# Windowed attention with a gated convolution layer on one core: 256-byte query and key runs, a block turn with unbroken writes, bias and row minimum in one operation, and a new order of the period

## The chip, the cores and the metric

The kernel runs on one core of a Trainium2 chip. The core has TensorE (PE, with its weight loads listed as PEld), VectorE (DVE), ScalarE (ACT), GpSimd (POOL), and SyncE (SP), which here only issues transfers. The metric is the device time of one execution in microseconds (us). The kernel before takes 621.04 us, the median of 3 runs (620.53 to 621.98).

## The reference, cut to what matters

Eight batches of 576 tokens, 8 heads of 64. Attention looks back at most 127 tokens and has a slope per head. A layer with a 3-tap convolution as its gate follows.

```python
scores = scale * np.matmul(q, k.transpose(0, 1, 3, 2))          # scale = 1/8
mask = (rel >= 0) & (rel < window)                              # window = 128
scores = np.where(mask, scores + bias[None], -1000000000.0)     # bias = -slope * distance
scores = scores - np.max(scores, axis=-1, keepdims=True)
attn = np.exp(scores)
attn = attn / (np.sum(attn, axis=-1, keepdims=True) + 1e-09)
x = np.matmul(attn, v)                                          # heads side by side: 512 wide
h = np.maximum(x @ w_in, 0.0)                                   # 512 -> 1024
conv_out = conv_w[0] * h[t-1] + conv_w[1] * h[t] + conv_w[2] * h[t+1]
out = h * (1 / (1 + np.exp(-conv_out))) @ w_out                 # 1024 -> 512
```

## The kernel before, in words

The 4608 tokens are cut into 36 tiles of 128. A tile's 8 heads are two halves of 4 (`u` is 0 or 1). The layer behind the attention works on chunks of 256 tokens, four steps per chunk, each step on 256 of the 1024 inner features. Every product with full precision is three passes of TensorE over a high and a low part of the numbers.

A whole program is an opening (tiles 0 to 7, weights, the first ten steps), fourteen periods of two tiles and four steps, and a tail. The order within these is written out by hand as strings of short codes, which `emit` plays off with a tile number t (even, 8 to 34) and a step number. Each engine keeps that order, and waits stand only where data or a buffer need them. So an instruction that waits holds up all that is behind it on its engine. The codes that the text speaks of, with the lines of the kernel before:

- LD: query and key loads (line 281, issued by SP). TQ: the 32x32 block turn on DVE (line 349). HQ, LQ: high part on ACT (line 362) and low part on POOL (line 369) of the turned tile.
- S: scores of a tile on PE (line 388), into four PSUM banks. MP: the previous tile's scores put in where the window needs them (DVE, line 461). MB: scale and bias added (line 487, DVE). RM: the row minimum of four heads (line 491, DVE). From tile 8 on, MB works on two heads at a time and RM on four. For tiles 0 to 7 one fused operation per head (line 480) does bias and minimum together.
- X: exponential with row sum (ACT, line 496). N: sum plus a constant, reciprocal and multiply (DVE, lines 507, 508, 514). T: transpose on PE (line 527). RL: its copy out of PSUM (ACT, line 535). SEL: the two window halves (POOL, lines 541 and 544). AV: product with the values (PE, line 560). XH, XL, XF: high and low part of the result (ACT line 576, DVE line 582), and one column copied round the ring for tiles divisible by 4 (DVE, line 587).
- UH: first product of a step (PE, line 619). HH: relu (ACT, line 631). Z: middle tap (ACT, line 637). CA, CB: the two side taps (DVE, line 652). TH: tanh (ACT, line 659). GT: gate (DVE, line 667). GH, GL: high and low part of the gated value (ACT line 679, POOL line 687). D: second product (PE, line 721). OB: the output copied out of PSUM and stored (ACT line 737, SP line 738).

PSUM holds five banks for scores, first products, transposes and AV results together, one for the convolution, two for the output. Where a tile or chunk straddles two batches, MP has a second operation and CA, CB are cut in two pieces.

In a load before, partition c of a block holds the four tokens 4c to 4c+3, which are 1024 unbroken bytes in memory. The turn must then write token 4c+m to column 4c+m, so that its writes step by four words:

```python
out=blks[tt][:, i].rearrange("p i g b (c m) -> p (i g) m b c", m=NB),
in_=raws[tt][:, i].rearrange("p i g (m b r) -> p (i g) m b r", m=NB, r=BK),
```

Of the kernel before, what the change touches and what calls it, by code (L numbers as in the profile page):

```python
# [8 lines left out]
F32 = mybir.dt.float32  # L9
# [13 lines left out]
def tile_alibi_window_attention_conv_glu(  # L23
# [10 lines left out]
    nc = tc.nc  # L34
    B, H, S, D = q.shape
# [3 lines left out]
    HU = 4  # L39
# [9 lines left out]
    cpool = ctx.enter_context(tc.tile_pool(name="cpool", bufs=1))  # L49
# [25 lines left out]
    spin(7, ones)  # L75
    neg = cpool.tile([P, 1], F32, name="neg")
    nc.vector.memset(neg, NEG)
    pos = cpool.tile([P, 1], F32, name="pos")
    nc.vector.memset(pos, -0.125 * NEG)

    def mask_from(name, conds):
        m = apool.tile([P, P], F32, name=name + "_f", tag="e", bufs=4)
# [194 lines left out]
    def load_blocks(t, dst, src):  # L277
        for r, b, s, n in segments(t):
            for j in range(NB):
                u, a = divmod(j, 2)  # L280
                nc.sync.dma_start(
                    out=dst[j * BK + r // NB : j * BK + (r + n) // NB],
                    in_=src[b, u * HU + a : (u + 1) * HU : 2, s : s + n, :].rearrange("g (c m) d -> c g (m d)", m=NB),
                )

    def load(t):
        if t >= TURN:
            raws[t] = apool.tile([P, 2, NG, NB * D], F32, name=f"rqk{t}", tag="rqk", bufs=3)
            if t == TURN:
                raws[t - 1, "k"] = apool.tile([P, 2, NG, NB * D], F32, name=f"rk{t - 1}", tag="rqk", bufs=3)  # L290
# [35 lines left out]
    def qkT_out(t, u):  # L326
        to = qkT_of(t)[:, t % SLOTS, u]
        ps = pts.pop((t, u)) if t < SPLIT else pts[t, u]
        if t < FIRST:
            nc.scalar.activation(out=to[:, 0], in_=ps[:, 0], func=AF.Copy, scale=-0.125)  # L330
            nc.scalar.copy(out=to[:, 1], in_=ps[:, 1])
        else:
            nc.scalar.copy(out=to, in_=ps)

    def qkT_rest(t, u):
        ps, hi = pts.pop((t, u)), as32(qkT_of(t)[:, t % SLOTS, u])
        low = qkT_low[:, t % SLOTS, u]
# [178 lines left out]

    def normal_act(t, u):
# [230 lines left out]
    def qk_rest(t):  # L748
# [61 lines left out]
    D-2 Z0.0 Z0.1 RM0.0 X0.0.0 X0.0.1 UH1.1 UH1.0 MB0.1.1 CA0.0 LQ1 RM0.1 CA0.1 X0.1.0 N0.0 X0.1.1 HH1 D-1 CB0.0 T0.0  # L810
    RL0.0 N0.1 T0.1 S1.0 CB0.1 RL0.1 TH0 TQ2 GT0 MP1.0.0 MB1.0.0 MP1.1.0 SEL0.0 AV-1 MP1.1.1 MB1.1.1 SEL0.1 AV0 GH0
    GL0 D0 XH-1 OB-2 XL-1 Z1.1 Z1.0 XH0 HQ2 LQ2 CA1.0 MB1.1.0 CA1.1 XL0 XF0 RM1.1 X1.1.0 CB1.0 MP1.0.1 CB1.1 X1.1.1
    TH1 LD5 MB1.0.1 UH2.1 UH2.0 HH2 Z2.0 Z2.1 GT1 OB0 GH1 N1.1 RM1.0 X1.0.0 X1.0.1 CA2.0 CA2.1 CB2.0 CB2.1 UH3.1
    UH3.0 T1.1 N1.0 GL1 TH2 GT2 RL1.1 LV3 SEL1.1 D1 HH3 Z3.1 Z3.0 TQ3 GH2 GL2 T1.0 RL1.0 SEL1.0 CA3.0 CA3.1 XF-1
    CB3.0 CB3.1 OB1 TH3 GT3
# [44 lines left out]
```

## Time and profile before

| what | value |
|---|---|
| median of 3 runs | 621.04 us |
| the profiled execution | 620.64 us |
| its span, first to last instruction | 618.9 us |
| PE / DVE / ACT / POOL busy | 97% / 86% / 71% / 47% |
| granted TensorE clock | full in all slices |
| chain that ended last | PE 59%, DVE 27%, ACT 5%, issue 5% |
| transfers | 47.39 MB, mean 77 GB/s |

The span is 1.7 us shorter than the execution. Busy shares are means over the whole span. A PE that counts as busy is not always at its peak rate, since the ends of its pipelined matmuls are modelled. So the chain and single stretches have to be read beside it.

### The profile page before, as it was taken

Reading aid. Unit: us, or ns where it says so; the run is one execution under the profiler, and the core shown is the slowest. Engines: PE = TensorE matmul, PEld = TensorE weight load, DVE = VectorE, ACT = ScalarE, POOL = GpSimd, SP = SyncE. Lnnn points to the kernel's source line nnn. Section 1 sums busy time; section 2 is a strip of 40 time slices with the busy share of each in tenths; the row PEclk is TensorE's granted clock in tenths of the full one; section 3 lists DMA queues with packets and bytes.
Section 4 is the critical chain, followed back from the end, with each engine's and each line's share of the span. In section 5 each row is a group of like instructions: output and inputs, shape, how many; then the busy total and the mean of one; then the engine's idle time right before and its main releaser. Section 6 shows DMA issues by size and latency. Waiting matters only on the chain.

```text
span 618.9 us, 14937 instructions
## 1 busy us (share of the span) xinstructions
PE 598.1 (97%) x5497; PEld 521.0 (84%) x5497; DVE 533.0 (86%) x1268; ACT 436.8 (71%) x1214; POOL 291.5 (47%) x362
## 2 busy tenths in 40 slices
PE   8999999999999999989999999999999999999997
PEld 7678877888897789879888888898989788989996
DVE  7999998899989998999898898889898999888553
ACT  6999977567776666758685768667777676676653
POOL 2679347553445354445354544434444535352411
PEclk9999999999999999999999999999999999999999
DMA  8997332312311222222322222221321120100001
GB/s 208 245 252 191 96 86 70 103 33 76 83 33 54 69 70 69 69 69 64 76 69 69 70 53 77 58 73 46 85 78 38 52 68 35 37 35 1 35 1 68
DMA packets 82012, 47.39 MB, mean 77 GB/s; under 512 B 61052, under 2 KB 75412, under 8 KB 81940
## 3 DMA queue, kind: packets, MB, share of 16 engines
q1 hardware_dynamic: 81940, 46.45, 27.7%
q8 instruction: 43, 0.70, 0.5%
q14 instruction: 29, 0.24, 0.1%
HBM read 36.99 MB, written 9.44 MB: 75 GB/s over the span
## 4 chain that ended last, share of the span: by engine, by line
PE 59%; DVE 27%; ACT 5%; issue 5%; POOL 1%; DMA 1%; SPq 0%; DVEq 0%; ACTq 0%
PE p L619 21%; PE o L721 20%; DVE zp L652 10%; PE av L560 7%; PE sc L388 5%; DVE sc L461 4%; PE pa L527 3%; DVE e L514 2%; DVE z L667 2%; DVE e L487 2%; ACT zp L637 2%; PE p L614 1%; DVE blk L349 1%; DMA rqk<-in_k_dram 1%; DVE st L491 1%
## 5 line engine op out<-in xcount | busy, mean ns | idle before, releaser
L619 PE MATMUL p<-ring,wi 128*128 128x256 f32 x1088 | 198.5, 284 | 3.7 <-DVE ring L587 3.7
L652 DVE SCALAR_TENSOR_TENSOR zp<-hh,cw,zp 128x256 f32<-128x256 f32 (+7 forms) x384 | 161.2, 420 | 28.8 <-ACT zp L637 20.9
L619 PEld LDWEIGHTS p<-ring,wi 128*128 128x128 f32 x1088 | 168.0, 188 | 9.0 <-issue 6.9
L687 POOL TENSOR_TENSOR gl<-z,gh 128x512 fp32r<-128x512 f32 x67 | 86.4, 1290 | 146.0 <-ACT gh L679 137.2
L619 PE MATMUL p<-ring,wl 128*128 128x256 f32 x544 | 152.5, 280 | 0.0
L496 ACT ACTIVATE e<-e,st 128x128 f32<-128x128 f32 x288 | 112.1, 392 | 29.3 <-DVE st L491 28.2
L721 PE MATMUL o<-wo,gh 128*128 128x512 f32 x270 | 110.1, 408 | 0.0
L721 PE MATMUL o<-wo,gl 128*128 128x512 f32 x270 | 107.3, 397 | 0.7 <-POOL gl L687 0.7
L721 PE MATMUL o<-wl,gh 128*128 128x512 f32 x270 | 105.4, 390 | 0.0
L619 PEld LDWEIGHTS p<-ring,wl 128*128 128x128 f32 x544 | 102.8, 189 | 0.0
L369 POOL TENSOR_TENSOR qkT_low<-blk,qkT 128x1024 fp32r<-128x1024 f32 (+1 forms) x28 | 66.2, 2368 | 35.6 <-ACT qkT L362 35.6
L637 ACT ACTIVATE zp<-hh,cw 128x256 f32<-128x256 f32 x144 | 69.0, 479 | 19.3 <-DVE z L667 9.5
L541 POOL TENSOR_SCALAR_AFFINE_SELECT rl<-rl 128x512 f32<-128x512 f32 x64 | 41.3, 645 | 82.0 <-ACT rl L535 82.0
L667 DVE SCALAR_TENSOR_TENSOR z<-zp,hh 128x512 f32<-128x512 f32 (+1 forms) x73 | 49.8, 682 | 31.4 <-ACT zp L659 30.5
L560 PE MATMUL av<-rl,rv 128*64 128x128 f32 x1088 | 65.6, 275 | 3.2 <-DVE e L487 1.7
L659 ACT ACTIVATE zp<-zp 128x512 f32<-128x512 f32 (+1 forms) x73 | 42.3, 579 | 34.1 <-DVE zp L652 26.1
L560 PEld LDWEIGHTS av<-rl,rv 128*64 128x64 f32 x1088 | 59.1, 137 | 7.9 <-issue 3.3
L721 PEld LDWEIGHTS o<-wo,gl 128*128 128x128 f32 x270 | 50.5, 187 | 17.1 <-POOL gl L687 6.0
L679 ACT CAST gh<-z 128x512 fp32r<-128x512 f32 (+1 forms) x69 | 41.6, 606 | 27.8 <-DVE z L667 27.8
L721 PEld LDWEIGHTS o<-wo,gh 128*128 128x128 f32 x270 | 50.7, 188 | 12.2 <-issue 1.4
L721 PEld LDWEIGHTS o<-wl,gh 128*128 128x128 f32 x270 | 50.8, 188 | 8.8
L535 ACT COPY rl<-pa 128x512 f32<-128x512 f32 x72 | 41.6, 585 | 22.0 <-PE pa L527 21.9
(120 smaller groups left out, 1064.0 us busy)
## 6 DMA issues: line engine op xcount, KB each, us to landing
out_dram<-ob SPq DMA_DIRECT2D x35, 256.0 KB, 2.4
rv<-in_v_dram SPq DMA_DIRECT2D x32, 256.0 KB, 3.2
rqk<-in_q_dram SPq DMA_DIRECT2D x96, 64.0 KB, 2.6
rqk<-in_k_dram SPq DMA_DIRECT2D x96, 64.0 KB, 1.9
wst<-in_moe_w_in_dram SPq DMA_DIRECT2D x8, 512.0 KB, 6.0
wst<-in_moe_w_out_dram SPq DMA_DIRECT2D x8, 512.0 KB, 4.6
rqk<-in_q_dram SPq DMA_DIRECT2D x7, 256.0 KB, 5.1
rqk<-in_k_dram SPq DMA_DIRECT2D x7, 256.0 KB, 5.4
```

The costliest lines, as they stand in the source:

```text
L369: eng.tensor_tensor(out=turned_of(qkT_low, s, i), in0=blks[tt][:, i], in1=hi, op=ALU.subtract)
L496: nc.scalar.activation(out=e[:, j, :], in_=e[:, j, :], func=AF.Exp, bias=st[:, 0, j : j + 1], scale=-1.0, accum_out=st[:, 1, j : j + 1],)
L535: nc.scalar.copy(out=rls[t, u][:, 0], in_=pas.pop((t, u)))
L560: nc.tensor.matmul(ps[a * D : (a + 1) * D, u * NG + g], vraw[tt][:, u * HU + j], rl[:, side, j], start=n == 0, stop=n == len(sides) - 1,)
L619: nc.tensor.matmul(ps, a[:, part], ring[:, i, cc, cols], start=cc == 0 and n == 0, stop=cc == NCC - 1 and n == 2)
L637: nc.scalar.activation(out=zps[s][:, ff, :], in_=hhs[s][:, ff, 1 : 1 + CW], func=AF.Copy, scale=cw[:, 1, f : f + 1])
L652: nc.vector.scalar_tensor_tensor(out=z[:, ff, a:cut], in0=hh[:, ff, a + kk : cut + kk], scalar=cw[:, kk, f : f + 1], in1=z[:, ff, a:cut], ...
L659: nc.scalar.activation(out=zps[s][:, ff], in_=zps[s][:, ff], func=AF.Tanh)
L667: nc.vector.scalar_tensor_tensor(out=zgs[s][:, ff], in0=zps[s][:, ff], scalar=1.0, in1=hhs[s][:, ff, 1 : 1 + CW], op0=ALU.add, op1=ALU.mult,)
L679: nc.scalar.copy(out=gs[s][0][:, ff], in_=zgs[s][:, ff])
L687: nc.gpsimd.tensor_tensor(out=gl, in0=zgs.pop(s), in1=as32(gh), op=ALU.subtract)
L721: nc.tensor.matmul(to, a[:, ff, ms], w[:, part], start=first and n == 0, stop=end and n == 2)
```

## The change

Four things change.

1. A query or key load of one block of heads becomes one transfer per head: partition c now takes tokens c, 32+c, 64+c and 96+c, each 256 bytes. A tile needs 16 transfers where it needed 8 (32 instead of 16 where it straddles two batches).
2. The block turn reads as before, but token 32m+c now belongs in column 32m+c, so that each 32x32 block is written as runs of 32 words.
3. The fused operation that tiles 0 to 7 used (bias and minimum in one instruction per head, plus the read of its accumulator) is used for all tiles, with the factor -0.125 in it. The separate row minimum (RM) is gone. The factor is no longer put into the queries of tiles 0 to 7, so their copy out of PSUM is one ACT instruction instead of two. A mask value that only those tiles used goes too.
4. The period's string is new. (`normal_pool`, code NP, is defined but no string uses it.)

```diff
     def load_blocks(t, dst, src):
         for r, b, s, n in segments(t):
             for j in range(NB):
-                u, a = divmod(j, 2)
-                nc.sync.dma_start(
-                    out=dst[j * BK + r // NB : j * BK + (r + n) // NB],
-                    in_=src[b, u * HU + a : (u + 1) * HU : 2, s : s + n, :].rearrange("g (c m) d -> c g (m d)", m=NB),
-                )
+                for g in range(NG):
+                    h = j // 2 * HU + 2 * g + j % 2
+                    nc.sync.dma_start(
+                        out=dst[j * BK : (j + 1) * BK, g, r // BK : (r + n) // BK],
+                        in_=src[b, h, s : s + n, :].rearrange("(m c) d -> c m d", c=BK),
+                    )
...
     def qkT_out(t, u):
-        if t < FIRST:
-            nc.scalar.activation(out=to[:, 0], in_=ps[:, 0], func=AF.Copy, scale=-0.125)
-            nc.scalar.copy(out=to[:, 1], in_=ps[:, 1])
-        else:
-            nc.scalar.copy(out=to, in_=ps)
+        nc.scalar.copy(out=to, in_=ps)
...
             nc.vector.transpose(
-                out=blks[tt][:, i].rearrange("p i g b (c m) -> p (i g) m b c", m=NB),
-                in_=raws[tt][:, i].rearrange("p i g (m b r) -> p (i g) m b r", m=NB, r=BK),
+                out=blks[tt][:, i].rearrange("p i g b (m c) -> p (i g) m b c", c=BK),
+                in_=raws[tt][:, i].rearrange("p i g m (b r) -> p (i g) m b r", r=BK),
             )
...
     def add_bias(t, u, a):
-        if t < FIRST:
-            for g in range(NG):
-                j = 2 * g + a
-                nc.vector.tensor_tensor_reduce(
-                    out=e[:, j, :], in0=s_cur[:, g, :], in1=bias[:, u * HU + j, :], scale=1.0, scalar=FAR,
-                    op0=ALU.add, op1=ALU.min, accum_out=st[:, 0, j : j + 1],
-                )
-            return
-        heads = heads_of(e, a)
-        b = heads_of(bias[:, u * HU : (u + 1) * HU], a)
-        nc.vector.scalar_tensor_tensor(out=heads, in0=s_cur, scalar=-0.125, in1=b, op0=ALU.mult, op1=ALU.add)
-
-    def rowmax(t, u):
-        e, st, pss = sms[t, u]
-        nc.vector.tensor_reduce(out=st[:, 0, :], in_=e, axis=mybir.AxisListType.X, op=ALU.min)
+        for g in range(NG):
+            j = 2 * g + a
+            nc.vector.tensor_tensor_reduce(
+                out=e[:, j, :], in0=s_cur[:, g, :], in1=bias[:, u * HU + j, :], scale=-0.125, scalar=FAR,
+                op0=ALU.add, op1=ALU.min, accum_out=st[:, 0, j : j + 1],
+            )
...
     PERIOD = """
-    LD4 UH0.1 UH0.0 S1.1 LV2 S0.0 S0.1 GH-1 HQ1 MP0.0.1 MP0.0.0 MB0.0.1 MB0.0.0 HH0 MP0.1.0 GL-1 MP0.1.1 OB-1 MB0.1.0
...
+    UH0.1 UH0.0 S0.0 MP0.0.0 S0.1 MP0.1.0 HH0 MP0.1.1 HQ1 Z0.0 D-2 Z0.1 GH-1 UH1.1 UH1.0 GL-1 MB0.0.0 X0.0.0 MP0.0.1
...
```

The order of PE's instructions and of POOL's is the same before and after, in all of the program. DVE, ACT and SP change. Three places follow.

DVE in the first half of a period, from the bias of tile 20 (`sc_0` to `sc_3` are its score banks, `e`, `st` its weights and statistics, `zp` the convolution). Before:

```order
L487 SCALAR_TENSOR_TENSOR e_0_4651<-sc_1_4596,bias 128x2x128
L487 SCALAR_TENSOR_TENSOR e_0_4651<-sc_0_4595,bias 128x2x128
L461 COPY_PREDICATED sc_2_4597<-m_prev,sc_2_4597 128x2x128
L461 COPY_PREDICATED sc_3_4598<-m_prev,sc_3_4598 128x2x128
L487 SCALAR_TENSOR_TENSOR e_1_4658<-sc_2_4597,bias 128x2x128
L491 TENSOR_REDUCE st_0_4652<-e_0_4651 128x4
L487 SCALAR_TENSOR_TENSOR e_1_4658<-sc_3_4598,bias 128x2x128
L652 SCALAR_TENSOR_TENSOR zp_4679<-hh_133,cw,zp_4679 128x256
L491 TENSOR_REDUCE st_1_4659<-e_1_4658 128x4
L652 SCALAR_TENSOR_TENSOR zp_4679<-hh_133,cw,zp_4679 128x256
L507 TENSOR_SCALAR st_0_4652<-st_0_4652 128x4
```

The same place now (the rows named ISA are the fused operation and, with one operand, the read of its accumulator):

```order
L465 ISA e_1_4782,st_1_4783<-sc_3_4730,bias 128x128
L465 ISA st_1_4783 128x1
L465 ISA e_1_4782,st_1_4783<-sc_3_4730,bias 128x128
L465 ISA st_1_4783 128x1
L635 SCALAR_TENSOR_TENSOR zp_4788<-hh_131,cw,zp_4788 128x256
L465 ISA e_1_4782,st_1_4783<-sc_2_4729,bias 128x128
L465 ISA st_1_4783 128x1
L465 ISA e_1_4782,st_1_4783<-sc_2_4729,bias 128x128
L465 ISA st_1_4783 128x1
L484 TENSOR_SCALAR st_0_4780<-st_0_4780 128x4
```

Two 4-head minimum operations are gone, each bias operation is two fused ones with their reads, and the reciprocal's first step (line 507, now 484) comes directly behind the bias.

DVE at the end of a period (tile 19 is the period's second tile, tile 21 is turned). Before:

```order
L491 TENSOR_REDUCE st_0_4339<-e_0_4338 128x4
L652 SCALAR_TENSOR_TENSOR zp_4449<-hh_131,cw,zp_4449 128x256 x2
L652 SCALAR_TENSOR_TENSOR zp_4449<-hh_131,cw,zp_4449 128x255 x2
L507 TENSOR_SCALAR st_0_4339<-st_0_4339 128x4
L508 RECIPROCAL st_0_4339<-st_0_4339 128x4
L514 TENSOR_TENSOR e_0_4338<-e_0_4338,st_0_4339 128x512
L667 SCALAR_TENSOR_TENSOR z_4505<-zp_4449,hh_131 128x512
L349 STREAM_TRANSPOSE blk<-rqk_3931 128x4x4x64
L652 SCALAR_TENSOR_TENSOR zp_4526<-hh_132,cw,zp_4526 128x256 x2
```

Now:

```order
L465 ISA st_0_4486 128x1
L338 STREAM_TRANSPOSE blk<-rqk_3961 128x4x4x2x32
L650 SCALAR_TENSOR_TENSOR z_4596<-zp_4488,hh_132 128x512
L447 COPY_PREDICATED sc_1_4387<-m_prev,sc_1_4387 128x2x128
L465 ISA e_0_4485,st_0_4486<-sc_1_4387,bias 128x128
L465 ISA st_0_4486 128x1
L465 ISA e_0_4485,st_0_4486<-sc_1_4387,bias 128x128
L465 ISA st_0_4486 128x1
L484 TENSOR_SCALAR st_1_4439<-st_1_4439 128x4
```

The turn of tile 21 has moved from behind the last gate of the period to the middle of its second half, ahead of the gate before.

ACT over the end of a period. Before:

```order
L535 COPY rl_1_4507<-pa_1_4494 128x512
L631 ACTIVATE hh_132<-p_4469 128x2x256
L637 ACTIVATE zp_4526<-hh_132,cw 128x256 x2
L679 CAST gh_4531<-z_4505 128x512
L535 COPY rl_0_4541<-pa_0_4536 128x512
L737 COPY ob_0_4549<-o_0_4190 128x512
L737 COPY ob_1_4552<-o_1_4191 128x512
L659 ACTIVATE zp_4526<-zp_4526 128x512
```

Now:

```order
L614 ACTIVATE hh_130<-p_4601 128x2x256
L518 COPY rl_1_4662<-pa_1_4639 128x512
L642 ACTIVATE zp_4591<-zp_4591 128x512
L720 COPY ob_0_4670<-o_0_4280 128x512
L720 COPY ob_1_4673<-o_1_4281 128x512
L620 ACTIVATE zp_4678<-hh_130,cw 128x256 x2
L518 COPY rl_0_4688<-pa_0_4681 128x512
L662 CAST gh_4690<-z_4668 128x512
L642 ACTIVATE zp_4678<-zp_4678 128x512
```

The two output copies now stand ahead of the last step's middle tap and of the copy `rl_0`, where they stood behind both.

## Rows read from the trace of the kernel before

**Rows 1.** Periods: length; PE, PEld, DVE, ACT, POOL busy; clock, DMA share, GB/s.
```profile
116.10:150.10 34.00, 32.02 (x298) 28.27 (x296) 30.27 (x70) 24.01 (x65) 16.00 (x18) 1.00 0.23 63
...
216.60:249.10 32.50, 31.85 (x323) 28.46 (x322) 28.91 (x65) 22.32 (x61) 14.87 (x18) 1.00 0.24 66
249.10:283.70 34.60, 32.32 (x322) 28.25 (x321) 31.90 (x71) 23.51 (x65) 16.11 (x20) 1.00 0.22 62
283.70:314.60 30.90, 30.90 (x306) 27.71 (x305) 27.22 (x57) 22.86 (x63) 14.41 (x17) 1.00 0.26 69
314.60:346.50 31.90, 31.90 (x322) 28.64 (x321) 27.10 (x58) 22.79 (x63) 15.42 (x18) 1.00 0.25 68
...
541.60:574.10 32.50, 31.95 (x323) 28.39 (x322) 27.38 (x68) 22.83 (x64) 14.00 (x19) 1.00 0.05 17
```
**Rows 2.** Chain of waits, 314.6 to 346.5, then 249.1 to 283.7: shares; start, us.
```profile
by line: PE o L721 36.4%; PE p L619 35.6%; PE av L560 11.4%; PE sc L388 11.1%; PE pa L527 5.8%
...
327.87 0.87 PE pa L527 x8
...
by line: DVE zp L652 18.7%; PE p L619 17.1%; issue 12.0%; PE o L721 8.6%; DVE e L487 7.2%; DVE sc L461 6.8%; DVE ring L587 6.7%; DVE e L514 4.0%; DVE z L667 4.0%; DVE ring L582 3.5%; DVE st L491 3.4%; DVE blk L349 2.8%; PE pa L527 1.9%; ACT
```
**Rows 3.** Groups by line and form on DVE: count, busy us, mean ns, idle before.
```profile
L349 DVE STREAM_TRANSPOSE blk<-rqk 128x1024 f32<-128x1024 f32 x27 | 55.7, 2064 | 0.5 <-issue 0.5
L667 DVE SCALAR_TENSOR_TENSOR z<-zp,hh 128x512 f32<-128x512 f32 x71 | 48.9, 689 | 30.4 <-ACT zp L659 29.4 <-POOL gl L687 0.7
...
L667 DVE SCALAR_TENSOR_TENSOR z<-zp,hh 128x256 f32<-128x256 f32 x2 | 0.8, 424 | 1.0 <-ACT zp L659 1.0
```
**Rows 4.** Order of time on DVE, 319.3 to 328: start, us, what.
```profile
320.06 0.75 DVE L487 SCALAR_TENSOR_TENSOR e<-sc,bias 128x256 f32<-128x256 f32 x2
...
321.72 0.67 DVE L491 TENSOR_REDUCE st<-e 128x4 f32<-128x512 f32 x1
322.31 0.42 DVE L487 SCALAR_TENSOR_TENSOR e<-sc,bias 128x256 f32<-128x256 f32 x1
...
324.11 0.17 DVE L507 TENSOR_SCALAR st<-st 128x4 f32<-128x4 f32 x1
...
326.07 0.69 DVE L514 TENSOR_TENSOR e<-e,st 128x512 f32<-128x512 f32 x1
```
**Rows 5.** Order of time on DVE, 97.4 to 99.4.
```profile
97.96 0.29 DVE L480 CUSTOM_DVE_ANT_0 e<-sc,bias 128x128 f32<-128x128 f32 x1
...
98.18 0.28 DVE L480 CUSTOM_DVE_ANT_0 e<-sc,bias 128x128 f32<-128x128 f32 x1
```
**Rows 6.** Order of time, 271 to 276, all engines.
```profile
271.70 2.38 POOL L369 TENSOR_TENSOR qkT_low<-blk,qkT 128x1024 fp32r<-128x1024 f32 x1 [2.54 <-ACT qkT L362]
271.81 2.30 DVE L587 CAST ring<-ring 128x8 fp32r<-128x8 f32 x1
...
274.25 0.47 PE L619 MATMUL p<-ring,wi 128*128 128x256 f32 x2 [1.25 <-DVE ring L587]
```
**Rows 7.** Line 507: ns min/median/max, first and last start, forms.
```profile
L507 DVE TENSOR_SCALAR st<-st x66: 151/164/1102, 14.2 to 571.5; 128x4 f32<-128x4 f32 x60, 128x8 f32<-128x8 f32 x6
```
**Rows 8.** Order of time on POOL, 319 to 325.
```profile
321.16 2.42 POOL L369 TENSOR_TENSOR qkT_low<-blk,qkT 128x1024 fp32r<-128x1024 f32 x1
```
**Rows 9.** Order of time on ACT, 314.6 to 323.
```profile
315.76 1.07 ACT L737 COPY ob<-o 128x512 f32<-128x512 f32 x2
...
319.08 0.62 ACT L679 CAST gh<-z 128x512 fp32r<-128x512 f32 x1 [0.83 <-DVE z L667]
319.61 1.04 ACT L362 CAST qkT<-blk 128x1024 fp32r<-128x1024 f32 x1
...
321.18 0.99 ACT L637 ACTIVATE zp<-hh,cw 128x256 f32<-128x256 f32 x2
```
**Rows 10.** Order of time on SP, 84 to 103, then DVE, 107 to 112.
```profile
98.05 1.72 SPq L281 DMA_DIRECT2D rqk<-in_q_dram  x4
...
109.05 2.01 DVE L349 STREAM_TRANSPOSE blk<-rqk 128x1024 f32<-128x1024 f32 x1
```

More of the change, by code (lines that the diff above doesn't have):

```diff
@@ L77, in tile_alibi_window_attention_conv_glu @@
     nc.vector.memset(neg, NEG)
-    pos = cpool.tile([P, 1], F32, name="pos")
-    nc.vector.memset(pos, -0.125 * NEG)
     def mask_from(name, conds):
@@ L122, in tile_alibi_window_attention_conv_glu @@
         nc.vector.tensor_scalar(
-            out=bias[:, h, :], in0=dist, scalar1=slope, scalar2=None, op0=ALU.mult
+            out=bias[:, h, :], in0=dist, scalar1=-8.0 * slope, scalar2=None, op0=ALU.mult
         )
@@ L279, in load_blocks @@
             for j in range(NB):
-                u, a = divmod(j, 2)
-                nc.sync.dma_start(
-                    out=dst[j * BK + r // NB : j * BK + (r + n) // NB],
-                    in_=src[b, u * HU + a : (u + 1) * HU : 2, s : s + n, :].rearrange("g (c m) d -> c g (m d)", m=NB),
-                )
+                for g in range(NG):
[4 more added lines that the diff above has]
+                    )
     def load(t):
         if t >= TURN:
-            raws[t] = apool.tile([P, 2, NG, NB * D], F32, name=f"rqk{t}", tag="rqk", bufs=3)
+            raws[t] = apool.tile([P, 2, NG, NB, D], F32, name=f"rqk{t}", tag="rqk", bufs=3)
             if t == TURN:
-                raws[t - 1, "k"] = apool.tile([P, 2, NG, NB * D], F32, name=f"rk{t - 1}", tag="rqk", bufs=3)
+                raws[t - 1, "k"] = apool.tile([P, 2, NG, NB, D], F32, name=f"rk{t - 1}", tag="rqk", bufs=3)
                 load_blocks(t - 1, raws[t - 1, "k"][:, 1], k)
@@ L337, in qkT_rest @@
         low = qkT_low[:, t % SLOTS, u]
-        if t >= FIRST:
-            nc.vector.tensor_tensor(out=low, in0=ps, in1=hi, op=ALU.subtract)
-            return
-        nc.vector.scalar_tensor_tensor(
-            out=low[:, 0], in0=ps[:, 0], scalar=-0.125, in1=hi[:, 0], op0=ALU.mult, op1=ALU.subtract
-        )
-        nc.vector.tensor_tensor(out=low[:, 1], in0=ps[:, 1], in1=hi[:, 1], op=ALU.subtract)
+        nc.vector.tensor_tensor(out=low, in0=ps, in1=hi, op=ALU.subtract)
     def turn(t):
@@ L410, in tile_alibi_window_attention_conv_glu @@
     sts = {}
-    def heads_of(x, a):
-        return x.rearrange("p (g a) k -> p a g k", a=2)[:, a]
     def scores(t, u):
@@ L461, in put @@
             nc.vector.copy_predicated(out=s_cur, mask=mask.unsqueeze(1).to_broadcast(shp), data=data)
-        negb = (pos if t < FIRST else neg).unsqueeze(2).to_broadcast(shp)
+        negb = neg.unsqueeze(2).to_broadcast(shp)
         if first == 0:
@@ L514, in normal, with normal_pool @@
         nc.vector.tensor_tensor(out=e, in0=e, in1=st[:, 2, :].unsqueeze(2).to_broadcast([P, HU, P]), op=ALU.mult)
+        es[t, u] = e
+    def normal_pool(t, u):
+        e, st, pss = sms[t, u]
+        recips(t, u)
+        nc.gpsimd.tensor_tensor(out=e, in0=e, in1=st[:, 2, :].unsqueeze(2).to_broadcast([P, HU, P]), op=ALU.mult)
         es[t, u] = e
@@ L754, in tile_alibi_window_attention_conv_glu @@
     TILE = {
-        "LD": load, "LH": load_half, "QU": qkT, "QV": qkT_out, "LV": loadv, "Q": qk, "QO": qk_out, "QL": qk_rest, "QM": qkT_rest, "TQ": turn, "HQ": qk_hi, "LQ": qk_lo, "MP": place, "MB": add_bias, "KH": keys_hi, "KL": keys_low, "KT": keys_top, "S": scores, "MA": merge, "RM": rowmax,
-        "X": lambda t, u, h: exps(t, u, range(h, HU, 2) if t < FIRST else range(2 * h, 2 * h + 2)),
-        "NR": recips, "N": normal, "NA": normal_act, "T": attnT, "RL": attn_out, "SEL": select, "AV": av, "XH": x_hi, "XL": x_lo, "XF": xfin,
+        "LD": load, "LH": load_half, "QU": qkT, "QV": qkT_out, "LV": loadv, "Q": qk, "QO": qk_out, "QL": qk_rest, "QM": qkT_rest, "TQ": turn, "HQ": qk_hi, "LQ": qk_lo, "MP": place, "MB": add_bias, "KH": keys_hi, "KL": keys_low, "KT": keys_top, "S": scores, "MA": merge,
+        "X": lambda t, u, h: exps(t, u, range(h, HU, 2)),
+        "NR": recips, "N": normal, "NA": normal_act, "NP": normal_pool, "T": attnT, "RL": attn_out, "SEL": select, "AV": av, "XH": x_hi, "XL": x_lo, "XF": xfin,
     }
@@ L808, in tile_alibi_window_attention_conv_glu @@
     PERIOD = """
-    LD4 UH0.1 UH0.0 S1.1 LV2 S0.0 S0.1 GH-1 HQ1 MP0.0.1 MP0.0.0 MB0.0.1 MB0.0.0 HH0 MP0.1.0 GL-1 MP0.1.1 OB-1 MB0.1.0
[L810 to L815, printed above, removed]
+    UH0.1 UH0.0 S0.0 MP0.0.0 S0.1 MP0.1.0 HH0 MP0.1.1 HQ1 Z0.0 D-2 Z0.1 GH-1 UH1.1 UH1.0 GL-1 MB0.0.0 X0.0.0 MP0.0.1
+    MB0.0.1 X0.0.1 CA0.0 MB0.1.1 X0.1.1 CA0.1 D-1 MB0.1.0 X0.1.0 LQ1 N0.0 HH1 T0.0 RL0.0 SEL0.0 N0.1 CB0.0 CB0.1 TH0
+    T0.1 RL0.1 TQ2 GT0 S1.0 MP1.1.1 HQ2 MB1.1.1 AV-1 MP1.1.0 GH0 SEL0.1 XH-1 XL-1 LD5 MP1.0.0 Z1.1 Z1.0 CA1.0 CA1.1
+    AV0 XH0 XL0 MB1.1.0 X1.1.1 GL0 D0 XF0 LQ2 LV3 X1.1.0 CB1.0 LD4 CB1.1 MB1.0.0 TH1 UH2.1 UH2.0 HH2 Z2.0 Z2.1 TQ3
+    GT1 MP1.0.1 MB1.0.1 UH3.1 GH1 GL1 N1.1 X1.0.0 CA2.0 UH3.0 X1.0.1 S1.1 T1.1 D1 CA2.1 HH3 OB0 LV2 CB2.0 CB2.1 RL1.1
+    TH2 XF-1 N1.0 GT2 OB1 SEL1.1 Z3.1 OB-1 Z3.0 T1.0 CA3.0 CA3.1 RL1.0 GH2 GL2 CB3.0 CB3.1 OB-2 TH3 GT3 SEL1.0
     """
```

2 lines of the change are left out of this document (removed).

## The prediction

> **What bounds the kernel now.** I read the stretches by period first, then the chain of waits inside two of them, and after that single lines. The fourteen periods run from 116.1 to 574.1 us, 458.0 in all [rows 1]; the first, the last and four between are shown. The reader should see three things there. The clock is full everywhere. The shortest period that does the usual work takes 31.9 with PE busy in all of it. A period with much VectorE work is longer: VectorE 27.1 goes with 31.9, 28.9 with 32.5, 30.3 with 34.0, 31.9 with 34.6. The chain says the same [rows 2]. In the 31.9 period every piece is a matmul. In the 34.6 period the chain runs through VectorE's convolution, bias, mask and turn, and matmuls have little over a quarter.
>
> So PE sets a floor, and VectorE is above it in part of the periods. The floor is 31.9 for eleven periods and 30.9 for the three that hold a tile without a predecessor [rows 1]: 351 + 93 = 443.6. What lies above it, 458.0 - 443.6 = 14.4 us, is the most that the periods can give. PE's order is unchanged, and so is the floor.
>
> **The turn.** 27 of 2064 ns [rows 3]. A two-input operation takes 689 ns for 512 columns and 424 for 256, so 1.035 ns a column; for 1024 columns that makes 689 + 512 x 1.035 = 1219 ns. The turn's 2064 is far above this rate, and its writes are what steps by four words. I take 1.22, the rate of that near row. The bounds: 2.06 (the step is not the reason) and 0.69 (the row of half the columns). Saving 2 x 0.85 = 1.7 us of VectorE a period.
>
> The Trainium skill (Vector Engine (DVE) Microarchitecture Reference, "5.2 Measured stream behaviour on trn2 (trn3 not measured)") says a port keeps full rate only on runs of two or more adjacent words, at 1.054 ns a column, and gives 1.71 with a destination that hops at every element. An estimate from that page is 1.15 us; the sum would be the same, since both leave VectorE below PE. The trace's 2.02 ns a column is above the page's hop figure, so the page does not prove that the step is all of it.
>
> **Bias and minimum.** Now, for four heads: two bias operations in 0.66 (the pair takes 0.75 with an overlap), and a minimum that holds the engine for 0.59, from 321.72 to 322.31 [rows 4]: 1.25. The fused operation starts every 0.22 (97.96 to 98.18), its read beside the next one [rows 5]: 0.88. Saving 0.37, four times a period: 1.5. Without the overlap a head costs 0.37 and the saving is nil. The exponentials also no longer wait for a minimum over all four heads.
>
> **What that is worth.** VectorE loses 1.7 + 1.5 = 3.2 us a period. The periods at 30 to 32 come to 27 to 29, where the rows show 0 to 0.6 above the floor [rows 1]. I keep 0.3 a period, 4.0 in all, for the mechanism in the next paragraph, and take 14.4 - 4.0 = 10.4.
>
> **The reciprocal and GpSimd.** One column copy on VectorE takes 2.30 because it started 0.11 after GpSimd's low-part subtraction and ended with it; PE waited 1.25 for it [rows 6]. The first step of the reciprocal (line 507) can suffer the same way: most of its 66 take 0.16, one 1.10 [rows 7]. Now it starts at 324.11, just clear of the subtraction that ends at 323.58 [rows 4, 8].
>
> The Trainium skill (SBUF — State Buffer, "Who interferes with whom") states the rule against this change: a VectorE operation in a two-port mode, or with two SBUF inputs, and a GpSimd operation exclude each other, and whoever issues first holds the ports for the whole instruction. The 2.30 agrees.
>
> The new order moves both sides. ScalarE's high part of the gate stands at 319.1 now, ahead of the turned tile's cast (1.04), the relu and the tap (0.99) [rows 9]; it moves behind them. With the second output copy (half of 1.07) ahead of it too, it starts about 2.0 later. GpSimd's subtraction follows it and ends at 323.58 + 2.0 = 325.6. VectorE reaches the reciprocal at 324.11 - 2 x 0.37 = 323.4, and so is held until 325.6. Two reciprocals and multiplies in a row take 2.1 (2.65 from 324.11 to 326.76 with one convolution of 0.5 between [rows 4]): done at 327.7. PE's transpose starts at 327.87 and needs the second half 0.44 later, at 328.3 [rows 2]. Room 0.6, so VectorE loses 2.2 us and PE nothing. Periods that cut the convolution in pieces use the room up; that is the 0.3.
>
> The same column copy should find GpSimd idle: the cast that the second subtraction of a period waits for moves ahead of the AV work.
>
> **Transfers.** A tile's issues double, 16 at 0.43 each: 6.9 us on SP [rows 10], twice in a period of 31.9, with the stores and value loads queued behind. Each load stands most of a period ahead of its turn, so this hides. It is dearest in the opening: 16 issues from 98.05 end at 104.9, 4.1 before the turn at 109.05 [rows 10]. If that cover were gone, a late turn would cost about 1 us, once.
>
> **Opening and tail.** The turns of tiles 8 (keys) and 9 stand in a VectorE-paced part: 0.85 and half as much again, 1.3. The merged query copy on ScalarE can only gain; I count nothing. The tail's code is unchanged.
>
> Sum: 620.64 (the profiled execution, its span 618.9 and 1.74 around it) - 10.4 - 1.3 = 608.9. The median of the runs shown is 0.4 above the profiled execution: **609.3 us**.
>
> **Rivals.**
> - *All hidden* (0.14). The held reciprocal never reaches PE: 620.64 - 14.4 - 1.3 + 0.4 = 605.3. For it: PE alone makes the chain at 27.1 of VectorE. Against: every period would have to run like the best.
> - *The lock eats part* (0.22). The multiply is shut out as well as the first step, and GpSimd's window selections catch a reciprocal in the second half too. T is then late by 0.6 a period, as much as the room worked out above: 609.3 - 4.0 + 14 x 0.6 = 613.7. For it: the 1.10 and the 2.30. Against: now nearly all of 66 escape. (The page of the Trainium skill named above states it for the multiply, which has two SBUF inputs.)
> - *The turn stays at 2.06* (0.07). VectorE loses 1.5 only; the heavy periods come to 29 to 30.5, where the rows show 0.6 to 2.1. Some 5 us more are kept, and the opening's 1.3: 615.6.
> - *Slower* (0.07). Both halves' reciprocals are caught in full, by the low-part subtraction (2.42) and by the selections, so that VectorE's savings turn into waiting and each T comes late. The whole gain is 15.7, 1.12 a period; from there it decides. At 1.4 a period: 620.64 + 0.4 - 15.7 + 14 x 1.4 = 624.9. For it: the room of 0.6 rests on ScalarE's order alone. Against: VectorE had 4.8 idle of 31.9 even before.
>
> The likeliest case, 609.3, has 0.50; its own range is 607 to 611.5. The range of 8 in 10 goes from 604.5 to 615.7 and leaves out the slower case and the ends of its neighbours. Below 0.2% (1.2 us) a measurement here cannot tell a change from none. All cases but the last are faster, 0.93; I move 0.02 of that, and 0.01 of the last case, to no change: 0.91 faster, 0.03 same, 0.06 slower.
>
> **What would show it.** Right: the turn near 1.2 us, the minimum gone and some 224 more fused operations with reads, periods of 31 to 32.5 whose chain is PE alone, the 2.3 us column copy gone, line 507 (484 now) at 1 to 2 us once a period, and PE's transposes not waiting for it. Wrong: a turn still near 2 us; PE waiting for the multiply before T in most periods; SP's stores or value loads late behind the doubled issues; or periods that stay at 33 with VectorE no longer busy.

## The result and the profile after

The changed kernel takes 613.88 us (median of 4 runs, 613.21 to 614.53), the kernel before 621.36 beside it: ratio 0.988, interval 0.9863 to 0.9898, so 7.5 us less. The profiled execution took 613.21 us; its span is 611.5. The forecast was 609.3, within 604.5 to 615.7. The direction and most of the mechanism came out. The size came short: about two thirds of the forecast gain.

The first view is the stretches by period, with the columns of [rows 1]: length; busy time of PE, PEld, DVE, ACT, POOL; clock, DMA share, GB/s. The last row is the tail.

```profile
114.80:148.20 33.40, 31.93 (x299) 28.33 (x298) 29.26 (x89) 23.66 (x65) 16.33 (x18) 1.00 0.28 69
...
179.80:213.00 33.20, 32.34 (x322) 28.41 (x321) 29.90 (x94) 22.55 (x63) 16.00 (x18) 1.00 0.26 64
...
308.40:340.20 31.80, 31.80 (x321) 28.54 (x320) 26.20 (x77) 22.64 (x63) 15.38 (x18) 1.00 0.33 81
...
468.20:501.30 33.10, 32.23 (x321) 28.39 (x320) 29.75 (x93) 22.51 (x63) 15.98 (x18) 1.00 0.26 65
...
565.70:611.50 45.80, 41.47 (x281) 37.13 (x279) 21.62 (x43) 21.42 (x44) 11.09 (x16) 0.98 0.10 35
```

The opening ends at 114.8 (before 116.1). The periods take 450.9 (before 458.0). The tail takes 45.8, where before it was 618.9 - 574.1 = 44.8. So the periods gave 7.1, the opening 1.3, and the tail took 1.0 back. The tail's clock of 0.98 comes from its last 1.4 us alone, when the matmuls are over. VectorE still shows near 30 in the long periods, but part of that is now waiting that counts as busy. The groups of VectorE by line and form show it (count; busy us, mean ns; idle before):

```profile
L491 DVE TENSOR_TENSOR e<-e,st 128x512 f32<-128x512 f32 x63 | 47.1, 750 | 2.1
L338 DVE STREAM_TRANSPOSE blk<-rqk 128x1024 f32<-128x1024 f32 x27 | 33.5, 1240 | 0.1
L484 DVE TENSOR_SCALAR st<-st 128x4 f32<-128x4 f32 x60 | 30.2, 504 | 0.6 <-ACT e L473 0.2
```

The turn (line 338) went from 2064 to 1240 ns [rows 3]. The reciprocal's first step (line 484) has a mean of 504 ns for four numbers a partition, while the median is 165. The next rows, from the order of time in the period of tile 20, show why (start, us, engine, what):

```profile
315.07 0.60 ACT L662 CAST gh<-z 128x512 fp32r<-128x512 f32 x1
...
317.14 2.40 POOL L358 TENSOR_TENSOR qkT_low<-blk,qkT 128x1024 fp32r<-128x1024 f32 x1
...
317.26 2.31 DVE L484 TENSOR_SCALAR st<-st 128x4 f32<-128x4 f32 x1
319.60 0.18 DVE L485 RECIPROCAL st<-st 128x4 f32<-128x4 f32 x1
319.82 0.69 DVE L491 TENSOR_TENSOR e<-e,st 128x512 f32<-128x512 f32 x1
```

The step starts 0.12 after GpSimd's subtraction and ends with it at 319.5. Before, it started at 324.11, behind the subtraction [rows 4, 8]. All fourteen periods now have such a hold. In this period it costs nothing. The chain of waits over it, by line, is matmuls alone:

```profile
by line: PE o L704 36.5%; PE p L602 35.7%; PE av L543 11.5%; PE sc L377 11.1%; PE pa L510 5.5%
```

In tile 12, a tile with a cut convolution, the same hold costs. The order of time there (POOL, DVE, PE):

```profile
189.17 2.41 POOL L358 TENSOR_TENSOR qkT_low<-blk,qkT 128x1024 fp32r<-128x1024 f32 x1
...
190.00 1.60 DVE L484 TENSOR_SCALAR st<-st 128x4 f32<-128x4 f32 x1
191.64 0.18 DVE L485 RECIPROCAL st<-st 128x4 f32<-128x4 f32 x1
191.85 0.69 DVE L491 TENSOR_TENSOR e<-e,st 128x512 f32<-128x512 f32 x1
...
192.88 0.69 DVE L491 TENSOR_TENSOR e<-e,st 128x512 f32<-128x512 f32 x1
...
193.71 0.63 PE L510 MATMUL pa<-ident_r,e 128*128 128x128 f32 x4 [0.20 <-DVE e L491]
```

Counted from the start of its period (179.8), the subtraction ends at 11.8; in tile 20 (308.4) it ends at 11.1. The second multiply ends at 13.8 against 13.1. That is the predicted room of 0.6, used up. What PE waits for, over the whole program (us in total, times, longest), sums it:

```profile
PE av L543 <- ACT rl L518: 1.9, 6, 0.4
...
PE pa L510 <- DVE e L491: 1.5, 6, 0.4
...
PE pa L510 <- DVE st L484: 1.0, 2, 0.7
...
PE av L543 <- POOL rl L527: 0.7, 1, 0.7
```

The first three are late transposes, and the AV products that are late behind them: 4.4 us, all but 0.3 of it in the periods of six tiles (8, 12, 16, 26, 30, 34), the ones with a cut convolution. The fourth is the tail.

The column copy is what the forecast said. It took up to 2298 ns in the kernel before, and now:

```profile
L570 DVE CAST ring<-ring x8: 171/172/483, 62.5 to 522.8; 128x8 fp32r<-128x8 f32 x8
```

### The profile page after: what moved, and what is told of

Its sections match the earlier page's. It is cut to its first block, busy times and chain, and to the rows that moved or that the text cites. A ratio compares the mean times of both kernels' runs of the same rounds, so it can differ in the third digit from the quotient of the medians.

```text
span 611.5 us, 15429 instructions
## 1 busy us (share of the span) xinstructions
PE 597.1 (98%) x5497; PEld 522.5 (85%) x5497; DVE 508.1 (83%) x1545; ACT 434.1 (71%) x1198; POOL 292.9 (48%) x362
## 4 chain that ended last, share of the span: by engine, by line
PE 72%; DVE 19%; ACT 4%; issue 2%; DMA 1%; SPq 1%; POOL 1%; ACTq 0%; DVEq 0%; POOLq 0%
PE o L704 24%; PE p L602 24%; PE av L543 9%; DVE zp L635 6%; PE sc L377 5%; PE pa L510 3%; DVE e L465 3%; DVE sc L447 3%; PE o L694 2%; DVE e L491 2%; DVE st L484 2%; ACT zp L642 1%; PE sc L421 1%; ACT zp L620 1%; SPq L280 1%
## 5 line engine op out<-in xcount | busy, mean ns | idle before, releaser
L465 DVE CUSTOM_DVE_ANT_0 e<-sc,bias 128x128 f32<-128x128 f32 x288 | 71.9, 288 | 3.4 <-DVE sc L447 0.2
L518 ACT COPY rl<-pa 128x512 f32<-128x512 f32 x72 | 41.7, 579 | 31.9 <-PE pa L510 31.8
L704 PEld LDWEIGHTS o<-wo,gh 128*128 128x128 f32 x270 | 50.7, 188 | 12.2 <-ACT zp L620 1.9
L614 ACT ACTIVATE hh<-p 128x512 f32<-128x512 f32 x67 | 39.4, 588 | 30.5 <-PE p L602 30.5
```

Source lines behind the costliest of these rows:

```text
L465: nc.vector.tensor_tensor_reduce(out=e[:, j, :], in0=s_cur[:, g, :], in1=bias[:, u * HU + j, :], scale=-0.125, scalar=FAR, op0=ALU.add, op ...
L518: nc.scalar.copy(out=rls[t, u][:, 0], in_=pas.pop((t, u)))
L704: nc.tensor.matmul(to, a[:, ff, ms], w[:, part], start=first and n == 0, stop=end and n == 2)
```

## The experiments

The experiments were timed in three sessions beside the kernel before (620.6, 620.5 and 620.9 us; the table's first row is the first of these). The changed kernel's row is the result above, with 621.4 beside it. Differences are taken against the kernel before of the same session. The period sums are of each profiled execution. "Copy" is the column copy; held means that it lasts over 1 us.

| kernel | median us | ratio, 95% interval | difference | periods us | copies held |
|---|---|---|---|---|---|
| before | 620.6 | 1 | | 458.0 | 3 |
| changed | 613.9 | 0.988 (0.9863 to 0.9898) | -7.5 | 450.9 | 0 |
| turn alone | 614.5 | 0.99 (0.9885 to 0.9916) | -6.1 | 451.9 | 3 |
| fused bias alone | 622.1 | 1.0014 (1.0004 to 1.0025) | +1.5 | 458.3 | 6 |
| both, old order | 616.9 | 0.9938 (0.9923 to 0.9952) | -3.7 | 454.0 | 6 |
| before, copy on ScalarE | 617.1 | 0.9942 (0.9927 to 0.9956) | -3.8 | 453.8 | 0 |
| fused alone, copy on ScalarE | 613.2 | 0.9877 (0.986 to 0.9894) | -7.7 | 450.0 | 0 |
| turn alone, copy on ScalarE | 610.3 | 0.9845 (0.983 to 0.9859) | -10.2 | 447.6 | 0 |
| both, old order, copy on ScalarE | 608.3 | 0.9804 (0.979 to 0.9817) | -12.2 | 445.6 | 0 |
| changed, low part first | 610.5 | 0.9836 (0.9818 to 0.9854) | -10.1 | 446.9 | 0 |
| changed, gate's cast back | 609.7 | 0.9824 (0.9811 to 0.9838) | -10.8 | 446.7 | 0 |
| changed, no addition | 609.6 | 0.982 (0.9807 to 0.9833) | -10.9 | 447.0 | 0 |
| changed, cast back and tail | 608.9 | 0.9807 (0.9788 to 0.9826) | -12.0 | 446.6 | 0 |

**The parts of the change, one by one**

The turn with its loads (the functions `load_blocks`, `load` and `turn` of the change, in the kernel before):

```diff
...
-out=blks[tt][:, i].rearrange("p i g b (c m) -> p (i g) m b c", m=NB),
+out=blks[tt][:, i].rearrange("p i g b (m c) -> p (i g) m b c", c=BK),
...
```

> The kernel before with only the loads and the turn of the change; old bias, row minimum and order. Theory (VectorE's load sets the long periods, whatever relieves it): the turn falls to 1.24 us, VectorE loses 1.65 us a period, the periods at 32.5 to 35.1 lose 0.5 to 1.5 each and the opening 1.3; the column copy held behind GpSimd (2.3 us in tiles 8, 12 and 16) stays. 615 to 617 us against 621.4. Rival (the new order makes the gain, the operations alone are hidden): 620 to 621.5, with a turn of 1.24 all the same.

It took 614.5, a little better than the theory. The turn alone brings most of what the whole change brings. Three column copies are still held.

The fused bias, with the old loads, turn and order:

```diff
...
-b = heads_of(bias[:, u * HU : (u + 1) * HU], a)
-nc.vector.scalar_tensor_tensor(out=heads, in0=s_cur, scalar=-0.125, in1=b, op0=ALU.mult, op1=ALU.add)
+for g in range(NG):
+    j = 2 * g + a
+    nc.vector.tensor_tensor_reduce(... scale=-0.125, scalar=FAR, op0=ALU.add, op1=ALU.min, accum_out=...)
```

> The kernel before with only the fused bias and minimum (old loads, turn and order; the minimum's places are empty). Theory (VectorE's load sets the long periods): VectorE loses about 1.5 us a period, 616 to 618 us; nothing in the opening. Rival (the fused operation costs as much as the pair it replaces, 0.37 us a head): 620.5 to 622.

It is not faster at all: 622.1, an excess of 1.5 that is near the bound of what can be told from none. In the profiles the periods are only 0.3 longer (458.3 against 458.0). The rest lies in the opening, 117.6 against 116.1, and the run below with the same opening and the copy moved took 116.2, so the 1.5 is not shown to be a cost of the fused bias. The time is the rival's, but not for its reason. Line 569 is the column copy of this kernel:

```profile
L569 DVE CAST ring<-ring x8: 170/1972/2323, 64.4 to 531.7; 128x8 fp32r<-128x8 f32 x8
...
  PE p L601: 7.5, 6
```

PE waits for it six times, 7.5 us in all, where before three copies were held (3.7 us). The three new ones are those of tiles 20, 24 and 32. In the kernel before, the copy starts there 0.01 to 0.02 us ahead of GpSimd's subtraction and runs freely (the period of tile 20 starts at 314.6):

```profile
335.95 0.17 DVE L587 CAST ring<-ring 128x8 fp32r<-128x8 f32 x1
335.97 2.42 POOL L369 TENSOR_TENSOR qkT_low<-blk,qkT 128x1024 fp32r<-128x1024 f32 x1 [2.96 <-ACT qkT L362]
336.04 0.68 DVE L491 TENSOR_REDUCE st<-e 128x4 f32<-128x512 f32 x1
```

With the fused bias it starts 0.08 behind the subtraction and is held (the period starts at 314.5):

```profile
335.82 2.37 POOL L357 TENSOR_TENSOR qkT_low<-blk,qkT 128x1024 fp32r<-128x1024 f32 x1 [2.95 <-ACT qkT L350]
335.90 2.32 DVE L569 CAST ring<-ring 128x8 fp32r<-128x8 f32 x1
```

So VectorE comes later to the copy here, by about 0.1 against the subtraction, although it has less to do in all. The two fused operations ahead of the copy take 0.42 where one bias operation took 0.33, and the minimum that they replace (line 491) stood behind the copy. What the fused bias saved in the periods, the three new holds took.

Both edits with the old order of the period (the row minimum's places are empty):

```diff
-    UH0.1 UH0.0 S0.0 MP0.0.0 S0.1 MP0.1.0 HH0 MP0.1.1 HQ1 Z0.0 D-2 Z0.1 GH-1 UH1.1 UH1.0 GL-1 MB0.0.0 ...
+    LD4 UH0.1 UH0.0 S1.1 LV2 S0.0 S0.1 GH-1 HQ1 MP0.0.1 MP0.0.0 MB0.0.1 MB0.0.0 HH0 MP0.1.0 GL-1 ...
```

> The changed kernel with the old order of the period: both edits of VectorE's work, no move. Theory (the new order takes away the held column copy, some 4 us over three periods, but brings the held reciprocal, some 4 us, and 1.0 us in the tail): 610 to 612 us, that is 2 to 4 below the changed kernel; the column copy still 1.2 to 2.3 us in tiles 8, 12 and 16; the reciprocal's first step near 0.16 in most periods; the tail from the last period's end 44.8 us. Rival (the order made most of the gain): 615 to 618.

616.9: the rival's time. My theory counted three held copies as in the kernel before, but there are six, the same as with the fused bias alone. The tail did not come out either: 45.4 and not 44.8, with no wait of PE in it. The order of time at one of the copies, and PE behind it:

```profile
396.55 2.38 POOL L358 TENSOR_TENSOR qkT_low<-blk,qkT 128x1024 fp32r<-128x1024 f32 x1 [2.96 <-ACT qkT L351]
396.62 2.33 DVE L570 CAST ring<-ring 128x8 fp32r<-128x8 f32 x1
...
399.10 0.48 PE L602 MATMUL p<-ring,wi 128*128 128x256 f32 x2 [1.26 <-DVE ring L570]
```

Adding the fused bias to the turn made the kernel slower by 2.4 us (614.5 to 616.9).

**The column copy taken out of the way**

Four kernels put the copy on ScalarE from tile 8 on and change nothing else:

```diff
-            nc.vector.tensor_copy(out=end, in_=as32(ring[:, :, :, 3:4]))
+            (nc.vector.tensor_copy if t < FIRST else nc.scalar.copy)(out=end, in_=as32(ring[:, :, :, 3:4]))
```

Both edits, old order:

> The changed kernel with the old order of the period (as in the run of the old order, 616.9 us) and the column copy of tiles divisible by 4 on ScalarE, from tile 8 on. Theory (in the old order six column copies of 1.07 to 2.33 us are held behind GpSimd's subtraction, and PE waits 1.42 for each): the six periods of 33.3 to 33.6 fall to 31.9, 607.5 to 609.5 us. Rival (the fused bias is slow in the old order for another reason): 614 to 617.

608.3, as the theory said. The copy on ScalarE takes 206 ns, and the six long periods are gone (periods 454.0 to 445.6, 1.4 for each):

```profile
L570 ACT CAST ring<-ring x7: 202/206/210, 137.8 to 518.9; 128x8 fp32r<-128x8 f32 x7
```

The turn alone:

> The kernel before with the new loads and turn only (614.5 us) and the column copy on ScalarE. Theory (three held copies, 1.42 each): 609.5 to 611.5 us, and 1 to 3 above the run that has the fused bias too, which shows what the fused bias is worth when nothing is held. Rival (the fused bias is worth nothing even then): equal to that run within 0.2%.

610.3, 2.0 above the kernel that has the fused bias too: the theory again.

The kernel before:

> The kernel before with one edit: the column copy of tiles divisible by 4 on ScalarE, from tile 8 on. Theory (three copies of 1.24 to 2.30 us are held, and PE waits 1.42 for each): 615.5 to 617 us against 620.5. Rival (VectorE's load takes the time back elsewhere): 619.5 to 620.5.

617.1, -3.8: just outside the narrow range, and of the theory's size (periods 458.0 to 453.8, three times 1.4).

The fused bias alone:

> The kernel before with the fused bias in all tiles (622.1 us) and the column copy on ScalarE. Theory (the fused bias frees some 1.5 us of VectorE a period, which the held copies ate, six of them at 1.42): 612.8 to 614.5 us, 2 to 4 below the kernel before with the same copy. Rival (the fused bias frees nothing): equal to that kernel within 0.2%.

613.2, -7.7. With nothing held, then, the fused bias is worth 3.9 us on the old turn (617.1 to 613.2) and 2.0 on the new one. The turn, whose runs lie in different sessions and are compared by the differences, is worth 6.4 without the fused bias (3.8 to 10.2) and 4.5 with it (7.7 to 12.2). Each is worth less where the other has already brought periods to PE's floor.

**The held reciprocal**

GpSimd's subtraction ahead of the gate's low part, in the changed kernel:

```diff
-Z0.1 GH-1 UH1.1 UH1.0 GL-1 MB0.0.0 ... MB0.1.0 X0.1.0 LQ1 N0.0
+Z0.1 GH-1 UH1.1 UH1.0 LQ1 GL-1 MB0.0.0 ... MB0.1.0 X0.1.0 N0.0
```

> The changed kernel with one GpSimd move: the low-part subtraction of the turned tile (2.4 us) ahead of the gate's low part (1.3 us); the other engines' orders are the same. Theory (the reciprocal and the multiply are held by that subtraction): it ends before VectorE comes to the reciprocal, the reciprocal's first step is back at 0.16, the transposes of tiles 8, 12, 16, 26, 30, 34 lose no time, 609 to 611 us against 613.9. Rival (VectorE is late in these tiles by its own work, and a held reciprocal hides): within 0.2% of the changed kernel, 612.8 to 615. Second rival (the gate's low part, now 2.4 us later, makes the second product wait): 614 to 620.

610.5, within the theory's range. Tile 12 in order of time; the subtraction is over before VectorE comes:

```profile
186.01 2.40 POOL L358 TENSOR_TENSOR qkT_low<-blk,qkT 128x1024 fp32r<-128x1024 f32 x1 [1.50 <-DVE sc L447]
188.37 1.30 POOL L670 TENSOR_TENSOR gl<-z,gh 128x512 fp32r<-128x512 f32 x1
...
189.64 0.18 DVE L484 TENSOR_SCALAR st<-st 128x4 f32<-128x4 f32 x1
```

In seven other periods the step meets the tail of the gate's low part or a selection instead and takes 0.35 to 0.88. The second rival did not show: no second product waits.

The gate's cast again ahead of the relu:

```diff
-MP0.1.0 HH0 MP0.1.1 HQ1 Z0.0 D-2 Z0.1 GH-1 UH1.1
+MP0.1.0 GH-1 HH0 MP0.1.1 HQ1 Z0.0 D-2 Z0.1 UH1.1
```

> The changed kernel with one ScalarE move taken back: the high part of the gate again ahead of the relu, the turned tile's cast and the middle tap. Theory (this move made GpSimd's subtraction late and so the reciprocal held): the subtraction ends some 2 us earlier, the reciprocal's first step is at most 0.5, 609.5 to 612 us. Rival (the subtraction waits for the turned tile's cast, not for the gate): no change, 612.5 to 614.5, the first step still 1.6 to 2.3.

609.7. This undoes one of ScalarE's moves and nothing else, and the hold on the reciprocal is gone from every period. Tile 12 again, whose period starts at 178.1 here:

```profile
186.11 2.40 POOL L358 TENSOR_TENSOR qkT_low<-blk,qkT 128x1024 fp32r<-128x1024 f32 x1
...
189.10 0.17 DVE L484 TENSOR_SCALAR st<-st 128x4 f32<-128x4 f32 x1
...
190.53 0.69 DVE L491 TENSOR_TENSOR e<-e,st 128x512 f32<-128x512 f32 x1
```

The subtraction ends at 10.4 from the period's start (before this edit 11.8), and the second multiply at 13.1 (13.8). Of the first three entries shown above, the list of what PE waits for keeps one wait for the reciprocal's step, 0.2 us in place of 1.0, and that lies in the opening; the other two are below 0.2 or gone. The periods are 450.9 - 446.7 = 4.2 us shorter. The period of tile 8 has 1.5 of this (33.4 to 31.9), and each of the other five tiles named above 0.5 to 0.6. All periods together (length; busy time of PE first, then as above):

```profile
114.60:561.30 446.70, 445.72 (x4410) 397.92 (x4409) 365.24 (x1185) 317.81 (x870) 214.59 (x246) 1.00 0.25 62
```

The addition left out:

```diff
-nc.vector.tensor_scalar(out=st[:, 2, :], in0=st[:, 1, :], scalar1=1e-9, scalar2=None, op0=ALU.add)
-nc.vector.reciprocal(out=st[:, 2, :], in_=st[:, 2, :])
+nc.vector.reciprocal(out=st[:, 2, :], in_=st[:, 1, :])
```

> The changed kernel without the addition of 1e-9 ahead of the reciprocal (left out in all tiles), so that the operation that is held now is gone. Theory (any VectorE operation that reads and writes SBUF there is shut out while GpSimd subtracts, so the next one takes the hold): the reciprocal or the multiply now lasts 1.5 to 2.7 in the same tiles, 613 to 614.5 us. Rival (only that form of operation is held): 609.5 to 611.5, the multiply at 0.69.

Here each theory got one half. The hold did go to the next operation that can be held, the multiply. The reciprocal itself never is: its longest of 66 is 198 ns, though it starts inside the subtraction 15 times. Tile 12, with its period at 179.6:

```profile
188.92 2.40 POOL L358 TENSOR_TENSOR qkT_low<-blk,qkT 128x1024 fp32r<-128x1024 f32 x1
...
189.74 0.17 DVE L484 RECIPROCAL st<-st 128x4 f32<-128x4 f32 x1
189.94 1.92 DVE L490 TENSOR_TENSOR e<-e,st 128x512 f32<-128x512 f32 x1
191.79 0.17 DVE L484 RECIPROCAL st<-st 128x4 f32<-128x4 f32 x1
191.99 0.69 DVE L490 TENSOR_TENSOR e<-e,st 128x512 f32<-128x512 f32 x1
```

But the time is the rival's, 609.6. VectorE loses about as long as before. Behind the subtraction's end (191.32), however, only the multiply's rest (0.54) and the second half are left to do, so the second multiply ends at 13.1 from the period's start and not at 13.8. About 0.2 of that is the step left out of the second half, which this run does not separate from the move of the hold. What decides is when the last multiply ends, not how long something is held.

**The tail**

The changed kernel with the gate's cast back, and in the last period alone:

```diff
-            emit(PERIOD, t, 2 * (t - FIRST) + 10)
+            last = PERIOD.replace(" GL2", "").replace(" SEL1.0", " SEL1.0 GL2")
+            emit(last if t == NT - 2 else PERIOD, t, 2 * (t - FIRST) + 10)
```

> The changed kernel with the gate's cast back ahead of the relu (609.7 us) and, in the last period alone, GpSimd's window selections of the last tile's first half ahead of the third gate's low part. Theory (in the tail PE waits 0.84 us for these selections, since no second product lies between the transpose and the AV product there): 608.5 to 609.2 us, a tail of 45.0. Rival (the next wait in the tail takes its place): 609.5 to 610.

608.9, as the theory said, 0.8 below the kernel without the tail's edit by the medians. The two were timed in different sessions, with 0.4 between their kernels before, so the tail itself is the better witness: 45.8 to 45.1. This is what it cures, in the changed kernel's order of time:

```profile
570.21 0.63 POOL L527 TENSOR_SCALAR_AFFINE_SELECT rl<-rl 128x512 f32<-128x512 f32 x1
...
570.90 1.97 PE L543 MATMUL av<-rl,rv 128*64 128x128 f32 x32 [0.68 <-POOL rl L527]
```

The two fastest versions are the old order with both edits and the copy on ScalarE (608.3), and the changed kernel with the cast back and the tail's edit (608.9). They cannot be told apart.

## Why the prediction was right in kind and short in size

- **What bounds it.** Right in kind. Periods with the usual work and no late transpose are PE alone, at 31.8 to 32.0 us. The floor summed from this was too low (below).
- **The turn.** Right: 1.22 predicted, 1.240 measured, in place of 2.064. An estimate from the page named there (Vector Engine (DVE) Microarchitecture Reference, section 5.2, of the Trainium skill) was 1.15; the trace is nearer to the row of the two-input operation. No run separates the step of the writes from the shorter runs of the loads.
- **The fused bias.** The saving was rightly taken as real, 2.0 to 3.9 us with no copy held. That in the old order it comes with three more held copies is a thing the prediction had no need of, since the copy moves; but it means that this edit, worth nothing in the old order, pays where the copy is out of the way, by the new order (613.9 against 616.9) or by ScalarE (608.3).
- **The column copy.** Right: free in the new order.
- **The held reciprocal.** Place and length right: once in every period, 0.43 to 2.31, against 1 to 2 and 2.2 in the prediction. It was caused by the move of the gate's cast, as the run with the cast put back shows. It reached PE in the six tiles with a cut convolution, as said. Cost: 4.2 us. I had kept 4.0.
- **The failed step: the floor of 443.6, with "I keep 0.3 a period, 4.0 in all" as all that stays above it.** The 4.0 were kept for the hold, and the hold took 4.2. But the floor itself was too low, and nothing was kept for that. With the hold gone, the periods still take 446.7, which is 3.1 above 443.6, and PE is busy in all but 1.0 of them (445.7). Of the three periods that the floor has at 30.9, only that of tile 18 takes this. Those of tiles 10 and 28 take 31.3 to 31.7 in every kernel here, 31.6 with the cast back: 1.5 of the 3.1. The periods of tiles 12 and 30 take 32.6 there with PE busy for 32.3 to 32.4: another 1.4. With the hold the periods take 450.9, 7.3 above, so 3.3 of the shortfall were not counted. The first part could have been read from the trace of the kernel before, where tiles 10 and 28 take 31.4 and 31.3 with PE busy for 31.3 and 31.2, and where PE's busy time in the fourteen periods comes to 446.0.
- **The second failed step: "The tail's code is unchanged."** The tail's string is, but what it starts from is not. ScalarE's cast of the third gate now stands behind two output copies, the middle tap and the copy `rl_0`. It starts 1.7 after the tail does, and started 0.1 after it before. First the kernel before, then the changed one (their tails start at 574.1 and 565.7):

```profile
574.23 0.60 ACT L679 CAST gh<-z 128x512 fp32r<-128x512 f32 x1
...
567.44 0.62 ACT L662 CAST gh<-z 128x512 fp32r<-128x512 f32 x1
```

GpSimd's low part waits for this cast, and the selections stand behind the low part, as they did before. In the tail no second product lies ahead of the AV product, and PE waits: 0.7 us of the 1.0. The other 0.3 lies behind the last matmul (3.65 us to the end, 3.3 before). With the old order and the new loads it is 3.9 there, and the tail 45.4 without any wait of PE. What makes this is open.

- **The opening.** 1.3 predicted, 1.3 seen (116.1 to 114.8). But kernels with the same opening gave 116.0, 114.6 and 117.0 too (low part first, cast back, cast back and tail), so one profile cannot confirm it.
- **Transfers.** Right: nothing waits. The loads of tile 9 are issued until 105.4, and VectorE comes to the turn at 108.31 with no idle time.
- **The sum.** 608.9, plus 3.3, plus 1.0, is 613.2, the profiled execution.
- **The rivals.** "The lock eats part" has the time, 613.7, but not quite the way. It asked for each transpose to be 0.6 late in every period. The loss comes in six tiles only: 0.5 to 0.6 in five of them, with the AV product's wait in it, and 1.5 in that of tile 8. The time agrees because the floor and the tail made up for the rest, which is luck. The multiply was shut out behind the first step in tile 8 only (2.65 us), and the selections slowed a multiply by 0.15 to 0.27 in seven periods.

## What to carry to other kernels

An edit that frees time on an engine, or moves it from behind an instruction to ahead of it, shifts the place of all that follows. There an instruction can start inside another engine's operation that excludes it, and 0.1 us was enough for this. So price an edit together with what its instructions then start beside. Measure a hold by when the last instruction ahead of the waiting engine ends, counted from the start of its period, and not by its length. Sum a floor from the busy time of each period, not from the best one of a kind, and keep an allowance for one thing only. Look, too, at the state in which a new order leaves the part behind the loop.

## What was not expected of the hardware

- A reciprocal of 128x4 is never held by GpSimd's subtraction (longest 198 ns of 66 in the kernel without the addition), while the addition of the same size waits up to 2311. The Trainium skill (SBUF — State Buffer, "Who interferes with whom") says that an operation with one SBUF input, outside the two-port modes, does not contend, and lists the tensor_scalar among those that can enter these modes. The runs agree with both.
- A multiply that GpSimd's subtraction or a selection holds in the periods ends 0.54 to 0.55 us after that operation, where one that runs freely takes 0.69.
- Three held copies became six by a shift of 0.1 us of the copy against the subtraction, though VectorE had less to do in all: the fused bias alone gained nothing (+0.3 us in the periods), and with the copy moved the same edit was worth 3.9.
